# Loading K and V of a decode attention block two heads at a time, each head on half of the partitions

## Chip, core and metric

The kernel runs on one core of a Trainium2 chip. The metric is the time of one execution on the device, in microseconds (us). The core has a matrix engine (TensorE, PE in the profile, with its weight loads as PEld), a vector engine (VectorE, DVE), a scalar engine (ScalarE, ACT), GpSimd (POOL), a sync engine (SyncE, SP) that issues the DMAs here, and 16 DMA engines that carry bytes from the DRAM (HBM) to the on-chip memory of 128 partitions.

## What is computed

One token `x` (640 numbers) goes twice through an attention block A and a mixer block B, with the same weights and the same caches both times. In code cut to what matters:

```
A(x):  q = layernorm(x) @ wq                       # 32 heads of 192
       k, v = cache[head, last 4096 rows, 192]     # one K and one V head per query head
       p = softmax(q . k / sqrt(192));  o = p @ v
       return o @ wo
B(x):  x1 = x + 0 (one position: the shifted paths are zero);  return x1 + gelu(layernorm(x1) @ w3) @ w4
x = x + A(layernorm(x));  x = x + B(layernorm(x));  and both once more
```

All tensors are bf16. The last 4096 rows of one head of K, or of V, are 4096 x 192 x 2 bytes = 1,572,864 bytes (1536 KB in the profile). Nearly everything that moves is K and V: 32 heads of each, for two layers.

## The kernel before

**Loads.** On-chip memory holds 11 buffers ("cells") of 128 partitions x 12,288 bytes. One head of K or V fills one cell: `load_k` (L128 to L131) and `load_v` (L133 to L145) read it as `(p j) d -> p (j d)`, so that partition p gets 32 consecutive rows, which are 12,288 consecutive bytes in DRAM. `take` (L114) pulls the next free cell from a queue, `give` returns one. The order of all loads is written out in advance by `layer_stream` (L203): K of the next group of four heads alternates with V of the current group, and `wo`, `w3` and `w4` stand between and behind. `need` (L247) issues loads in that order. SP carries them all on one queue; each waits until the instructions that used its cell last are done. In layer 1, K of heads 0 to 6, V of heads 2 and 3 and a part of V of head 4 are not loaded again, since layer 0 keeps them on the chip.

**Scores.** Layer 0 takes its groups from head 31 downwards, layer 1 from head 0 upwards. VectorE turns each K head in four pieces in 32-bit words (`transpose_quart`, L358 to L378), PE multiplies them by the query (`scores`, L441 to L454). The query stands in `Qblk`, a block that is zero outside of the columns of one head, so the four heads of a group add into one PSUM tile (`qproj_steps`, its `block` at L430 writes the four heads with one VectorE instruction).

**Softmax.** `softmax_steps` (L471) takes maxima, exponentiates on ScalarE, turns P on VectorE (L510), swaps it into place with 16 matmuls (`swap`, L521), copies the result to `PT` on ScalarE (L524) and sums the rows (L526).

**PV.** `pv` (L558) runs 16 matmuls for each head (L567), with two columns of `PT` as weights and 384 columns of V as moving data, and then one VectorE transpose of the result (L574). `o_fold` (L576) folds four partial sums into the head's output with small matmuls and one ScalarE scaling.

**Order.** The four compute engines and SP run in the order in which the Python code records instructions (the schedule is manual); `attention` (L639 on) interleaves the next group's scores with the current group's PV. The mixer follows each layer.

The loads' source patterns, before, are one line each:

```python
t = take(("k", layer, h))
nc.sync.dma_start(t[:], A_k_cache[0, h, s0:Sk, :].rearrange("(p j) d -> p (j d)", p=P))
```

Of the kernel before, what the change touches and what calls it, by code (L numbers as in the profile page):

```python
# [17 lines left out]
P = 128  # L18
# [17 lines left out]
def kernel(  # L36
# [39 lines left out]
    NKEEP, NCELL = 7, 11  # L76
# [13 lines left out]
    cells = ctx.enter_context(tc.tile_pool(name="cells", bufs=1))  # L90
# [15 lines left out]
    kx = const.tile([P, VN], BF16, name="kx")  # L106

# [3 lines left out]
    free = deque(range(NCELL))  # L111
    cell_of = {}

    def take(key):  # L114
        i = free.popleft()
        cell_of[key] = i
        return cells.tile([P, FREE], BF16, tag=f"cell{i}", name=f"cell{i}")

    def give(key):
        free.append(cell_of.pop(key))  # L120
# [7 lines left out]
    def load_k(layer, h):  # L128
        t = take(("k", layer, h))
        nc.sync.dma_start(t[:], A_k_cache[0, h, s0:Sk, :].rearrange("(p j) d -> p (j d)", p=P))  # L130
        return t  # L131

    def load_v(layer, h):  # L133
        t = take(("v", layer, h))
        src = A_v_cache[0, h, s0:Sk, :].rearrange("(p j) d -> p (j d)", p=P)
        cut = (2 * VW,) if h == VP else (FREE - VN,) if h == VX else ()
        if layer == 1 and h in GROUPS[layer][-1][-2:]:
            cut = FREE // 2,
        i = 0
        for e in cut + (FREE,):  # L140
            kept_v = h == VP or h == VX and i > 0
            if layer == 0 or not kept_v:
                nc.sync.dma_start(v_pair(t, h, i, e - i), src[:, i:e])
            i = e
        return t  # L145
# [23 lines left out]
    def load_w3(layer):  # L169

        t = take(("w3", layer))
        src = B_w3.rearrange("(k p) f -> p k f", p=P)
        n = W3C if layer == 0 else W3C // 2
        for k in range(0, W3C, n):
            nc.sync.dma_start(t[:, k * F:(k + n) * F].rearrange("p (k f) -> p k f", f=F), src[:, k:k + n, :])
        if layer == 0:
            nc.sync.dma_start(wx_sb[:, 0:(ND - W3C) * F].rearrange("p (k f) -> p k f", f=F), src[:, W3C:, :])
        return ([t[:, k * F:(k + 1) * F] for k in range(W3C)]
                + [wx_sb[:, k * F:(k + 1) * F] for k in range(ND - W3C)])

    def load_w4(layer):

        t = take(("w4", layer))
        blocks = [t[:, k * D:(k + 1) * D] for k in range(W4C)]
        x0 = (ND - W3C) * F
        blocks += [wx_sb[:, x0 + k * D:x0 + (k + 1) * D] for k in range(NF - W4C)]
        pairs = B_w4.rearrange("(k p two) n -> p k (two n)", p=P, two=2)
        ones_ = B_w4.rearrange("(k p two) n -> p k two n", p=P, two=2)
        h = W4C // 2
        n = h if layer == 0 else h // 2  # L190
        for k in range(0, h, n):
            nc.sync.dma_start(t[:, 2 * k * D:2 * (k + n) * D].rearrange("p (k n) -> p k n", k=n), pairs[:, k:k + n, :])
        nc.sync.dma_start(blocks[2 * h], ones_[:, h, 0, :])
        if layer == 0:
            nc.sync.dma_start(blocks[2 * h + 1], ones_[:, h, 1, :])
            rest = NF // 2 - h - 1
            nc.sync.dma_start(wx_sb[:, x0 + D:x0 + D + 2 * rest * D].rearrange("p (k n) -> p k n", k=rest),
                              pairs[:, h + 1:, :])
        return blocks
# [3 lines left out]
    def layer_stream(layer):  # L203
        groups = GROUPS[layer]
        seq, later = [], []

        def k_item(hh):
            if layer == 0 or hh >= NKEEP:
                seq.append(("k", layer, hh))

        def v_item(hh):
            if (layer, hh) == (1, VC):
                return
            if (layer, hh) == (1, VP):
                later.append(("v", layer, hh))
                return
            seq.append(("v", layer, hh))

        if layer == 0:
            for hh in groups[0]:  # L220
                k_item(hh)
        for gi, cur in enumerate(groups):
            nxt = list(groups[gi + 1]) if gi + 1 < len(groups) else []
            late = gi + 2 >= len(groups)
            for i, hh in enumerate(cur):
                if nxt:
                    k_item(nxt.pop(0))
                if nxt and late and i == 2:
                    k_item(nxt.pop(0))
                v_item(hh)  # L230
                if later and seq[-1] == ("k", layer, NKEEP):
                    seq.append(later.pop())
                if layer == 0 and gi + 1 == len(groups) and i < 2:
                    seq.append(("wo", layer, groups[gi + i - 1][0] // QH))
            if gi + 2 < len(groups) and gi >= layer:
                seq.append(("wo", layer, cur[0] // QH))
        if layer == 1:
            for g in groups[-2:]:
                seq.append(("wo", layer, g[0] // QH))
        seq.append(("w3", layer))  # L240
        seq.append(("w4", layer))
        return seq
# [19 lines left out]
    ones = const.tile([P, P], F32, name="ones")  # L262
    nc.vector.memset(ones[:], 1.0)
# [16 lines left out]
    nc.vector.reduce_sum(lo[:], ident[:, 0:64], axis=AX.X)  # L280
    maskq = const.tile([P, 4], F32, name="maskq")
# [38 lines left out]
    def ln_center(x, rowsum):  # L320

        mean_ps = psm.tile([P, 1], F32, tag="psm")
        nc.tensor.matmul(mean_ps[:], lhsT=ones[:], rhs=rowsum[:, 0:1], start=True, stop=True)
# [10 lines left out]
        def total():  # L334
            var_ps = psm.tile([P, 1], F32, tag="psm")
            nc.tensor.matmul(var_ps[:], lhsT=ones[:], rhs=ssq[:, 0:1], start=True, stop=True)
# [21 lines left out]
    def transpose_quart(layer, h, q):  # L358
# [5 lines left out]
        Ku = Kn[:].bitcast(U32).rearrange("p (j y b) -> p j y b", j=NJ4, b=32)  # L364
# [4 lines left out]
        else:  # L369
            if area[0] is None:  # L370
                area[0] = take(("area", layer))
# [8 lines left out]
    def qproj_steps(c, xc, part=None, row=None):  # L380
# [6 lines left out]
        def project():  # L387
            need("wq", 0, ND - 1)
# [41 lines left out]
        def block():  # L430
            nh = n * P // Dh
            h0 = 4 * (t0 - c * QT) // NCOL
            diag = Qblk[:, c % 2].rearrange("p (h r) -> p h r", h=QH)[:, h0:h0 + nh, 0:QHEAD]
# [37 lines left out]
    def softmax_steps(n, ST_ps, sc):  # L471
# [25 lines left out]
        def spread_max():  # L497
            nb_ps = psm.tile([P, 1], F32, tag="psm")
            nc.tensor.matmul(nb_ps[:], lhsT=held["w"],  # L499
                             rhs=ones[0:1, 0:1], start=True, stop=True)  # L500
# [14 lines left out]
        def swap():  # L515
            ng = NGK // NT
            PT_ps = psm.tile([P, n, NJ4, NGK], F32, tag="psm")
            src = held["PrT"].rearrange("p (g j i) -> p i j g", g=ng, j=NJ4)
# [4 lines left out]
            PT = big.tile([P, n, NJ4 * NGK], BF16, name="PT")  # L523
            nc.scalar.copy(PT[:].rearrange("p h c -> p (h c)"), PT_ps[:].rearrange("p h j g -> p (h j g)"))  # L524
            l_ps = psm.tile([P, QH], F32, tag="psm")
            nc.tensor.matmul(l_ps[:], lhsT=ones[:], rhs=held["lh"][:], start=True, stop=True)  # L526
            held["lps"] = l_ps
            return PT
# [29 lines left out]
    def pv(layer, h, hq, PT, mid=None):  # L558
# [3 lines left out]
        NB = NJ4 * NGK // 2  # L562
        for i in range(NB):
            if mid is not None and i == NB // 2:
                mid()
            r = 32 * (i % 4)
            nc.tensor.matmul(O_ps[r:r + 2, :], lhsT=PT[:, hq, 2 * i:2 * i + 2],  # L567
                             rhs=v_pair(V, h, 2 * i * Dh, 2 * Dh), start=(i < 4), stop=(i >= NB - 4))
# [3 lines left out]
        else:  # L572
            give(("v", layer, h))
        nc.vector.transpose(o_sb[:], O_ps.rearrange("p (e a c) -> p e c a", e=2, c=NA))  # L574

    def o_fold(h, oT, rl, add=False):  # L576
        r = slice(32 * (h % QH), 32 * (h % QH) + 32)
        oT_ps = psm.tile([P, NA], F32, tag="psm")
        if not add:
            for e in range(2):  # L580
                nc.tensor.matmul(oT_ps[r, :], lhsT=Lq[:], rhs=o_sb[:, e, :, e], start=(e == 0), stop=(e == 1))  # L581
# [3 lines left out]
        nc.vector.tensor_add(o2[:], o_sb[:, 0, :, 0], o_sb[:, 1, :, 1])  # L585
# [53 lines left out]
    def attention(layer, x_cur, rs_cur, x_new, z_new, rs_new, ss_new):  # L639
# [18 lines left out]
        def S(h, half, ST_ps, hq):  # L658
# [6 lines left out]
            if half == 1 and layer == 0 and h == last_plain:  # L665
                give(("area", layer))
                area[0] = None

        def add_y(y_ps, n):
            y_new = x_new if n == 0 else sm.tile([P, ND], F32, name="y_acc")  # L670
            if n == 1:
# [5 lines left out]
                def center():  # L677
                    nm_ps = psm.tile([P, 1], F32, tag="psm")
                    nc.tensor.matmul(nm_ps[:], lhsT=ones[:], rhs=rs[:, 0:1], start=True, stop=True)
# [17 lines left out]
        qa, qb = (qproj_steps(groups[0][0] // QH, xc, part) for part in (0, 1))  # L697
# [6 lines left out]
        q1 = qproj_steps(groups[1][0] // QH, xc)  # L704
# [27 lines left out]
        for gi, cur in enumerate(groups):  # L732
            nxt = list(enumerate(groups[gi + 1])) if gi + 1 < len(groups) else []
            ST_n = None
            if nxt:
                part_max, turn_max, full_max, spread_max, turn_p, swap, recip = softmax_steps(len(cur), ST, sc)
                ST_n = next_scores()
                if layer == 1 and gi == 0:
# [3 lines left out]
                    q = qproj_steps(groups[2][0] // QH, xc)  # L742
# [17 lines left out]
                else:  # L760
# [14 lines left out]
                    if gi + 2 < len(groups):  # L775
                        q = qproj_steps(groups[gi + 2][0] // QH, xc, row=q_row if gi in rows else None)
# [33 lines left out]
            for hq, h in order:  # L810
                pv(layer, h, hq, PT, fold)
                if final:
# [5 lines left out]
                    if hq < QH - 2:  # L818
                        o_fold(h, oT, rl)
                    else:  # L820
                        def fold(h=h):
                            o_fold(h, oT, rl)
# [10 lines left out]
                elif hurry and hq == 2:  # L833
                    S(h3, 1, ST_n, q3)
                    steps = softmax_steps(len(cur), ST_n, sc)
# [7 lines left out]
                o_fold(h, oT, rl, len(groups) - 4 > gi >= 2 * layer)  # L843
# [14 lines left out]
    def mixer(layer, x_cur, z, rs_cur, ss_cur, x_new, rs_new):  # L858
# [5 lines left out]
        nc.tensor.matmul(s1_ps[:], lhsT=ones[:], rhs=rs_cur[:, 0:1], start=True, stop=True)  # L864
        s2_ps = psm.tile([P, 1], F32, tag="psm")
        nc.tensor.matmul(s2_ps[:], lhsT=ones[:], rhs=ss_cur[:, 0:1], start=True, stop=True)
# [35 lines left out]
        give(("w3", layer))  # L902
# [31 lines left out]
        give(("w4", layer))  # L934
# [51 lines left out]
```

## Time and profile before

| what | value |
|---|---|
| time, median of 3 runs (lowest, highest) | 525.11 us (524.75, 526.35) |
| span of the profiled execution | 522.9 us |
| taken as lying around the span (525.11 less 522.9) | 2.2 us |
| DMA issues, bytes read | 159, 216.47 MB |
| PE, DVE, ACT, POOL busy | 330.3, 294.6, 49.5, 4.0 us |
| one L574 transpose, one L567 matmul | 582 ns, about 510 ns |

The profiled execution's own time outside of the profiler is not given; its span is 522.9 us, and the median of the runs stands 2.2 us above it. The profile has a page with the engines' busy time, the span in 40 slices with what the DMA engines moved in each, the DMA queues, the chain of work that ended last, and groups of instructions. A list of DMA issues names each load with its size and the time from its issue to its landing. Below that list lie the records of single DMA packets, each with its size and its duration.

### The profile page before, as it was taken

Reading aid. Unit: us, or ns where it says so; the run is one execution under the profiler, and the core shown is the slowest. Engines: PE = TensorE matmul, PEld = TensorE weight load, DVE = VectorE, ACT = ScalarE, POOL = GpSimd, SP = SyncE. Lnnn points to the kernel's source line nnn. Section 1 sums busy time; section 2 is a strip of 40 time slices with the busy share of each in tenths; the row PEclk is TensorE's granted clock in tenths of the full one; section 3 lists DMA queues with packets and bytes.
Section 4 is the critical chain, followed back from the end, with each engine's and each line's share of the span. In section 5 each row is a group of like instructions: output and inputs, shape, how many; then the busy total and the mean of one; then the engine's idle time right before and its main releaser. Section 6 shows DMA issues by size and latency. Waiting matters only on the chain.

```text
span 522.9 us, 9589 instructions
## 1 busy us (share of the span) xinstructions
PE 330.3 (63%) x4146; PEld 195.5 (37%) x4146; DVE 294.6 (56%) x589; ACT 49.5 (9%) x175; POOL 4.0 (1%) x16
## 2 busy tenths in 40 slices
PE   2057668666665566767655866667675666647675
PEld 2023334333332333434333544334343333425344
DVE  2067656666574664556624264766576866654722
ACT  1000101010010100001011101001010101001011
POOL 2000000000000000000000000000000000000000
PEclk9995656567677776576555567657787865766755
DMA  8999999999999999999999999999999999999996
GB/s 345 429 424 425 423 426 427 423 424 423 427 421 428 424 422 428 423 423 423 423 399 398 388 425 427 424 424 423 426 423 424 426 423 426 421 427 425 420 410 237
DMA packets 23949, 217.08 MB, mean 415 GB/s; under 512 B 2532, under 2 KB 3044, under 8 KB 8420
## 3 DMA queue, kind: packets, MB, share of 16 engines
q1 hardware_dynamic: 23908, 216.48, 99.0%
q8 instruction: 32, 0.52, 0.4%
q14 instruction: 9, 0.07, 0.0%
HBM read 216.47 MB, written 0.00 MB: 414 GB/s over the span
## 4 chain that ended last, share of the span: by engine, by line
DMA 43%; PE 27%; DVE 25%; issue 2%; ACT 2%; SPq 1%; DVEq 0%; ACTq 0%
PE ST_ps L451 11%; DVE cell_3304 L375 9%; PE O_ps L567 8%; DVE cell_277 L375 8%; DMA cell_1925<-in_A_k_cache_dram 6%; DMA cell_4933<-in_A_k_cache_dram 5%; DMA cell_1629<-in_A_k_cache_dram 5%; DMA cell_1329<-in_A_k_cache_dram 5%; DMA cell_4637<-in_A_k_cache_dram 5%; DMA cell_5324<-in_A_v_cache_dram 5%; DMA cell_275<-in_A_k_cache_dram 4%; DVE o_sb L574 2%; DMA cell_2478<-in_A_v_cache_dram 2%; DMA cell_2690<-in_A_v_cache_dram 2%; DMA cell_5423<-in_B_w_dram 2%
## 5 line engine op out<-in xcount | busy, mean ns | idle before, releaser
L451 PEld LDWEIGHTS <-Qblk 128*16 128x16 bf16 x1536 | 86.1, 113 | 178.6 <-issue 151.1
L451 PE MATMUL ST_ps<-cell_277,Qblk 128*16 128x256 bf16 x600 | 70.1, 392 | 50.9 <-DVE cell_277 L375 34.3
L574 DVE STREAM_TRANSPOSE o_sb<-O_ps 128x384 f32<-128x384 f32 x64 | 37.2, 582 | 112.4 <-PE O_ps L567 112.3
L451 PE MATMUL ST_ps<-cell_3304,Qblk 128*16 128x256 bf16 x600 | 67.3, 382 | 43.5 <-DVE cell_3304 L375 28.3
L567 PEld LDWEIGHTS <-PT 128*2 128x2 bf16 x1024 | 47.2, 102 | 21.8 <-issue 11.3
L510 DVE STREAM_TRANSPOSE o_sb<-o_sb 128x256 bf16<-128x256 bf16 x16 | 7.1, 445 | 34.1 <-ACT o_sb L505 25.0
L582 ACT ACTIVATE oT<-oT_ps,rl 32x6 bf16<-32x6 f32 x40 | 10.3, 258 | 163.5 <-PE oT_ps L581 157.1
L581 PEld LDWEIGHTS oT_ps<-o_sb,Lq 128*32 128x32 f32 x160 | 13.2, 145 | 19.9 <-issue 16.1
L581 PE MATMUL oT_ps<-o_sb,Lq 128*32 128x6 f32 x160 | 13.9, 196 | 10.4 <-DVE o_sb L574 9.9
L587 ACT ACTIVATE oT<-oT_ps,rl 32x6 bf16<-32x6 f32 x24 | 6.2, 258 | 108.4 <-PE ST_ps L451 93.7
L405 PE MATMUL qT_ps<-xc,wq_sb 128*128 128x1 bf16 x210 | 7.2, 165 | 13.4 <-DMA wq_sb<-in_A_wq_dram 12.5
L419 DVE TENSOR_TENSOR Xq<-qT_ps,maskq 128x24 bf16<-128x24 f32 (+1 forms) x18 | 2.8, 157 | 18.3 <-PE qT_ps L405 18.3
L521 PE MATMUL PT_ps<-o_sb,Eq 128*32 128x32 bf16 x256 | 7.2, 237 | 9.2 <-DVE o_sb L510 4.0
L394 PE MATMUL qr_ps<-wq_sb,xc 128*1 128x384 bf16 x90 | 12.8, 433 | 0.0
L521 PEld LDWEIGHTS <-Eq 128*32 128x32 bf16 x256 | 5.5, 111 | 18.9 <-issue 18.8
L405 PEld LDWEIGHTS <-wq_sb 128*128 128x128 bf16 x210 | 6.8, 104 | 14.8 <-DMA wq_sb<-in_A_wq_dram 13.6
L502 ACT COPY nb_sb<-nb_ps 128x1 f32<-128x1 f32 x16 | 2.5, 159 | 97.6 <-PE nb_ps L499 97.6
L526 PE MATMUL l_ps<-lh,ones 128*128 128x4 f32 x32 | 8.5, 336 | 4.9 <-ACT PT L524 4.9
L499 PEld LDWEIGHTS nb_ps<-ones,o_sb 1*128 1x128 f32 x32 | 7.6, 292 | 7.4 <-issue 5.5
L526 PEld LDWEIGHTS l_ps<-lh,ones 128*128 128x128 f32 x32 | 7.1, 275 | 7.5 <-ACT PT L524 7.1
L499 PE MATMUL nb_ps<-ones,o_sb 1*128 1x1 f32 x32 | 8.9, 345 | 1.5 <-DVE o_sb L491 1.5
L426 PE MATMUL Qrep_ps<-Xq,Lb 128*128 128x24 bf16 (+1 forms) x18 | 3.2, 179 | 10.4 <-DVE Xq L419 10.1
(376 smaller groups left out, 533.2 us busy)
## 6 DMA issues: line engine op xcount, KB each, us to landing
wq_sb<-in_A_wq_dram SPq DMA_DIRECT2D x5, 1536.0 KB, 12.7
cell_275<-in_A_k_cache_dram SPq DMA_DIRECT2D x1, 1536.0 KB
cell_309<-in_A_k_cache_dram SPq DMA_DIRECT2D x1, 1536.0 KB, 26.4
cell_346<-in_A_k_cache_dram SPq DMA_DIRECT2D x1, 1536.0 KB, 27.1
cell_376<-in_A_k_cache_dram SPq DMA_DIRECT2D x1, 1536.0 KB
cell_444<-in_A_k_cache_dram SPq DMA_DIRECT2D x1, 1536.0 KB, 30.8
cell_503<-in_A_v_cache_dram SPq DMA_DIRECT2D x1, 1536.0 KB, 30.8
cell_505<-in_A_k_cache_dram SPq DMA_DIRECT2D x1, 1536.0 KB, 30.8
```

Of the source, the lines that this page charges most:

```text
L375: nc.vector.transpose(Tu, Ku[:, :, q * NY:(q + 1) * NY])
L394: nc.tensor.matmul(qr_ps[32 * i:32 * i + 1, :], lhsT=xc[:, kc:kc + 1], rhs=wq_sb[:, kc, t0 * P + i * N:t0 * P + (i + 1) * N], start=(kc == ...
L405: nc.tensor.matmul(qT_ps[:, tl:tl + 1], lhsT=wq_sb[:, kc, t * P:(t + 1) * P], rhs=xc[:, kc:kc + 1], start=(kc == 0), stop=(kc == ND - 1))
L451: nc.tensor.matmul(ST_ps[r:r + QW, :].rearrange("p (g i) -> p g i", g=ng), lhsT=Q[:, n, :], rhs=T4[:, :, f, :, t], start=(hq == 0 and n == ...
L499: nc.tensor.matmul(nb_ps[:], lhsT=held["w"], rhs=ones[0:1, 0:1], start=True, stop=True)
L510: nc.vector.transpose(held["PrT"], held["Pr"])
L521: nc.tensor.matmul(PT_ps[32 * m:32 * (m + 1), :, :, ng * q:ng * (q + 1)], lhsT=Eq[:, q, :], rhs=src[:, m:QW:NM], start=True, stop=True)
L526: nc.tensor.matmul(l_ps[:], lhsT=ones[:], rhs=held["lh"][:], start=True, stop=True)
L567: nc.tensor.matmul(O_ps[r:r + 2, :], lhsT=PT[:, hq, 2 * i:2 * i + 2], rhs=v_pair(V, h, 2 * i * Dh, 2 * Dh), start=(i < 4), stop=(i >= NB - 4))
L574: nc.vector.transpose(o_sb[:], O_ps.rearrange("p (e a c) -> p e c a", e=2, c=NA))
L581: nc.tensor.matmul(oT_ps[r, :], lhsT=Lq[:], rhs=o_sb[:, e, :, e], start=(e == 0), stop=(e == 1))
L582: nc.scalar.activation(oT[r, :], oT_ps[r, :], ACTF.Copy, scale=rl[r, 0:1])
```

## The change

K and V of heads 8 to 31 in layer 0, and of heads 12 to 31 in layer 1, load in pairs. One DMA brings heads h and h + 1: h to partitions 0 to 63 and h + 1 to partitions 64 to 127, 24,576 bytes on each partition, into two neighbouring cells. Those are 24 heads x 2 + 20 heads x 2 = 88 head loads, in 44 pairs. The cells become slices of one tile, `arena`, and the cell of each load comes from a list that is written out. Each of the two cells then holds one half of both heads, and what worked on a head works on such a half-half cell:

- `block` writes the query of a pair group so that one cell's scores come out for two heads, with four smaller VectorE instructions for a group instead of one. The zeros around them are at other places in pair groups, so GpSimd clears half of `Qblk` again where the kind of group changes.
- `swap_pair` takes the place of `swap`: 16 matmuls with other strides, then two ScalarE instructions that scale by 1 or 0 (`lo`, `hi`) instead of one copy, so that `PT` has twice the columns, half of them zero on each half of the partitions.
- `pv` uses four columns of `PT` as weights instead of two, adds both cells of a pair into the same PSUM rows, and transposes the result once for a pair.
- `o_fold` folds both heads of a pair behind the second.
- The last V pair of layer 1 loads in three cuts (12,288, 6,144 and 6,144 bytes of each partition); before, the last two V heads loaded in two halves each.

As built, there are 115 DMA issues instead of 159 for the same 216.47 MB. VectorE has 22 fewer of the 128x384 transposes (42 instead of 64), and of the `Qblk` writes 44 small ones and 6 of the old kind instead of 18 of the old kind, and one more of 128x1; ScalarE has 22 `PT` instructions and 5 copies instead of 16 copies; GpSimd has 4 more clears of 128x400. The numbers of matmuls and of weight loads are the same.

```diff
-    NKEEP, NCELL = 7, 11
+    NKEEP, NCELL, NSINGLE = 7, 11, (8, 12)
...
-    cells = ctx.enter_context(tc.tile_pool(name="cells", bufs=1))
+    arena = const.tile([P, NCELL * FREE], BF16, name="arena")
...
+    def is_pair(layer, h):
+        return h >= NSINGLE[layer]
+    def take(key, n=1):
+        i = plan.popleft()
+        for c in range(i, i + n):
+            free.remove(c)
+            cell_of[(*key[:-1], key[-1] + c - i)] = c
+        return arena[:, i * FREE:(i + n) * FREE]
...
     def load_k(layer, h):
+        if is_pair(layer, h):
+            return load_pair("k", A_k_cache, layer, h)
         t = take(("k", layer, h))
...
+    def load_pair(kind, cache, layer, h):
+        t = take((kind, layer, h), 2)
+        src = cache[0, h:h + 2, s0:Sk, :].rearrange("h (r j) d -> h r (j d)", r=P // 2)
+        cuts = (FREE, 3 * FREE // 2) if (kind, layer, h) == ("v", 1, H - 2) else ()
+        i = 0
+        for e in cuts + (2 * FREE,):
+            nc.sync.dma_start(t[:, i:e], src[:, :, i:e])
+            i = e
+        for e in range(2):
+            loaded[kind, layer, h + e] = t[:, e * FREE:(e + 1) * FREE]
+        return loaded[kind, layer, h]
...
+            if (layer, c) in ((0, NSINGLE[0] // QH - 1), (0, NSINGLE[0] // QH - 2),
+                              (1, NSINGLE[1] // QH), (1, NSINGLE[1] // QH + 1)) and not part:
+                nc.gpsimd.memset(Qblk[:, c % 2], 0.0)
...
+            if is_pair(layer, c * QH):
+                r = held["r"][:, :].rearrange("p (h f) -> p f h", h=nh)
+                m = blkm[:, :].rearrange("p (c g) -> p c g", c=2).unsqueeze(1).broadcast_to([P, NCOL, 2, 2])
+                for h in range(nh):
+                    v, e = h0 + h, h % 2
+                    x = QHEAD * v + 8 * (v // 2) + 2 * e
+                    rows = Qblk[:, c % 2, x:x + QHEAD].rearrange("p (f x) -> p f x", x=QW)[:, :, 0:8]
+                    nc.vector.tensor_tensor(
+                        out=rows.rearrange("p f (c g) -> p f c g", c=2)[:, :, :, 0:2],
+                        in0=r[:, :, h - e:h - e + 2].unsqueeze(3).broadcast_to([P, NCOL, 2, 2]), in1=m, op=ALU.mult)
+                return
...
+        def swap_pair():
...
+            for c, side in enumerate((lo, hi)):
+                nc.scalar.activation(PT[:, :, :, c], PT_ps[:].rearrange("p h j (g e) -> p h (j g) e", e=2),
+                                     ACTF.Copy, scale=side[:, 0:1])
...
-            nc.tensor.matmul(O_ps[r:r + 2, :], lhsT=PT[:, hq, 2 * i:2 * i + 2],
-                             rhs=v_pair(V, h, 2 * i * Dh, 2 * Dh), start=(i < 4), stop=(i >= NB - 4))
+            nc.tensor.matmul(O_ps[r:r + M, :], lhsT=PT[:, hq, i, :],
+                             rhs=v_pair(V, h, 2 * i * Dh, 2 * Dh), start=(i < 4 and not (paired and h % 2)),
+                             stop=(i >= NB - 4 and not (paired and h % 2 == 0)))
...
+        if paired and h % 2 == 0:
+            return
         nc.vector.transpose(o_sb[:], O_ps.rearrange("p (e a c) -> p e c a", e=2, c=NA))
```

## The prediction

> **What bounds the kernel now.** I read the 40 slices first, then the DMA queues, the chain that ended last, and the list of DMA issues.
>
> ```profile
> DMA  8999999999999999999999999999999999999996
> GB/s 345 429 424 425 423 426 427 423 424 423 427 421 428 424 422 428 423 423 423 423 399 398 388 425 427 424 424 423 426 423 424 426 423 426 421 427 425 420 410 237
> DMA packets 23949, 217.08 MB, mean 415 GB/s; under 512 B 2532, under 2 KB 3044, under 8 KB 8420
> ...
> q1 hardware_dynamic: 23908, 216.48, 99.0%
> ```
>
> The 16 DMA engines are busy in every slice but the first and the last, and move 423 to 428 GB/s throughout, apart from the three slices at the change of layers. So the loads bound the kernel: 424 GB/s over 16 engines is 26.5 GB/s for each engine, and one head of 1.573 MB takes 1.573 / 424 = 3.71 us. No compute engine comes near.
>
> ```profile
> PE 330.3 (63%) x4146; PEld 195.5 (37%) x4146; DVE 294.6 (56%) x589; ACT 49.5 (9%) x175; POOL 4.0 (1%) x16
> ...
> DMA 43%; PE 27%; DVE 25%; issue 2%; ACT 2%; SPq 1%; DVEq 0%; ACTq 0%
> ```
>
> The chain names PE and DVE too, but only because a load waits for the cell that they free while seven others are in flight (a load issued at 173.34 us landed 29.22 us later, eight times 3.71 us). The queue on the 16 engines never runs dry.
>
> **How many engines does a load use?** This decides the case. Each DMA engine that takes part in a load closes it with one packet of 4 bytes; the packet records hold 2,522 of these on q1. There are 159 issues. Two of them are unlike the rest:
>
> ```profile
> wx_sb<-in_A_x_dram SPq DMA_DIRECT2D x1, 1.2 KB
> out_dram<-Lb SPq DMA_DIRECT2D x1, 1.2 KB
> ```
>
> They have five rows of 256 bytes each, and all others have 128. 157 x 16 + 2 x 5 = 2,522, and with the ten rows of 256 bytes that is the 2,532 "under 512 B" of the page exactly. With 16 engines for these two it would be 2,554, with one 2,524. So the outer count of a load's access pattern sets its engines: 128 rows run on 16, five rows on five.
>
> The new load's destination still has 128 rows. Its source, `h (r j) d -> h r (j d)`, has an outer count of 2: two heads lie 6,291,456 elements apart and their 64 rows can't be joined into one step. No row of before has unlike outer counts on its two sides. The bounds are 16 engines (the destination's 128 decides) and 2 (the source's 2 decides). My reason: an engine reads and writes the same piece, so a load can hardly be cut finer than its coarser side. The nearest row, the load of `x`, is the only load with fewer than 16 source rows, and it ran on as many engines as it had rows. I take 2.
>
> [...]
>
> **The price of a pair on two engines.** One engine moves 64 rows of 24,576 bytes. The packet records have 12,288 bytes in 462 ns (median of 15,232) and 7,680 in 294 ns (1,792). Doubling gives 924 ns for 24,576 bytes, the slope between the two gives 462 + 12,288 x (168 / 4,608) = 910. I take 917: 64 x 917 = 58.7 us for a pair, where two heads took 7.42 us. Does an engine get faster when the other 14 are idle? Packets of 2,560 bytes take 106 ns with 16 or more packets in flight and 102 ns with 5 to 12, as the queue drains at the end; 1,280 bytes take 55 ns in both. So at most 4% are to be had.
>
> **The sum.** From the span I take the 88 heads at the old price and add 44 pairs at the new one. All other loads (216.47 less 138.41 MB) stay as they are, on 16 engines, and queue behind the pairs on the two busy ones as before:
> 522.9 - 88 x 3.71 + 44 x 58.7 = 522.9 - 326.5 + 2,582.8 = 2,779.2 us. With the 2.2 us by which the median of the runs exceeds the span: **2,781 us**, 5.3 times before.
>
> Does the queue stay full? A pair waits for two neighbouring cells, an added wait on SP, and behind it wait all later loads and through them everything. By the waits of the built program, at least three further loads are already in flight whenever a pair lands. One pair takes 58.7 us, in which all engines together have less than 15 us of work for two heads (PE 330.3 us for 128 head steps of K and V, 2.6 us for one; DVE 2.3). So the wait ends long before its turn, and costs nothing.
>
> **The other edits** lie under these loads. Each with its row:
> - VectorE: 22 transposes at L574 go, 22 x 582 ns = 12.8 us less. 44 small `Qblk` writes (128x24) come, between 155 ns (the 128x24 write at L419) and 247 ns (the old 128x96 one), taken at 160: 7.0 us more, while 12 old ones at 247 ns or less go, 3.0 less. Net about 9 us less of 294.6.
> - ScalarE: 22 `PT` instructions for 11 copies of 266 ns: 2.9 us more, 0.27 us on each pair group's way from P to PV.
> - GpSimd: 4 clears of 128x400, between 0.41 us (33x384, L728) and 0.77 us (128x800, L303); the `Qblk` write of that group waits for it, and scores behind that, once each.
> - PE: as many matmuls. 704 weight loads of 4 columns instead of 2: between 102 ns (2 columns) and 113 ns (16 columns), at most 7.7 us in all, beside matmuls of 510 ns. The 176 matmuls of `swap_pair` read and write with other strides: 237 ns each by the old row, at worst doubled, 42 us in all.
> - The first fold of a pair moves behind the second head: one fold of about 1 us later at the end. The tail holds 17.6 us behind the last V landing (505.28 to 522.9) and keeps them: `wo`, `w3` and `w4` still load on 16 engines behind it.
> - SP: 44 issues fewer at 0.33 to 0.49 us; it waits most of the time already.
> If the cover were gone (loads free), all these together would be some 50 us at worst; beside 58.7 us for each pair they are nothing.
>
> **Rivals.**
> 1. *All 16 engines take the pairs* (the destination's 128 decides), and the change does what it can: eight rows of 24,576 bytes on each engine, 910 to 924 ns, against sixteen of 462: 44 x 8 x 0 to 14 ns = 0 to 4.9 us less. The dip at the change of layers (three slices near 395 instead of 424) holds another 3 x 13.07 x 29 / 424 = 2.7 us that other prefetching could win. This gives 517.5 to 525, about 522 us: the other side, faster. It decides from the point where the closing packets show 16 per pair. For it: 128 partitions are written. Against: the `x` load's five.
> 2. *Sixteen engines, but the pairs stall.* A wait for two free cells lets the queue run dry. Priced at one more pair time (7.4 us) at each of the 11 pair groups: 525 + 82 = 607 us. Against: three loads in flight behind each.
> 3. *An uneven split gives 8 engines* (each head's 64 rows cut further): 16 rows each, 14.7 us for a pair: 522.9 - 326.5 + 646.8 + 2.2 = 845 us. No row shows such a cut.
>
> **How the numbers follow.** Two engines 0.87 (2,781 us); sixteen and faster or alike 0.07; sixteen with stalls 0.02; eight 0.04. For the two-engine case the low end is 4% off the pairs' 2,582.8 us (103) and 910 ns rather than 917 (20): 2,658, rounded out to 2,640. The high end takes the mean packet of 466 ns doubled, 932 ns (42 us more), and a gap of 2 us between any two pairs (88 us): 2,911, rounded to 2,920. This range holds about 0.93 of its case, 0.81 of all, so it needs no other case in it. A measurement can tell about 0.3% from no change: faster by more than that 0.05, within 0.02, slower 0.93.
>
> **What would show it.** Right: the GB/s line near 53 in the slices of pairs and 420 where single heads load, a mean DMA share near two sixteenths there; 44 pairs, or 46 issues with the last one's cuts, that close with two 4-byte packets each; rows of 24,576 bytes at 910 to 930 ns; PE, DVE and ACT with nearly the same busy time, waiting for DMAs. Wrong: slices at 420 GB/s all through (rival 1), or two-engine loads whose packets are clearly shorter than 880 ns, so that an engine alone outruns its share. A split of the 24,576-byte rows into smaller packets would move the packet count and hardly the sum.

## The result and the profile after

The changed kernel takes 2,811.34 us (median of 4 runs, 2,810.24 to 2,811.71), the kernel before 524.99 us (median of 4). The ratio is 5.3525, with a 95% interval of 5.3449 to 5.3601. 2,781 us were forecast, in a range of 2,640 to 2,920. The profiled execution has a span of 2,808.5 us. All ratios here are taken over the runs within 1.5% of their kernel's fastest.

The slices of the changed kernel, with the busy share of the DMA engines, what they moved, and the packet counts:

```profile
DMA  3111111111111111112239621111111111111113
GB/s 150 54 54 54 65 54 54 65 54 54 54 65 54 54 65 54 54 65 93 90 111 361 264 103 51 54 66 54 54 54 65 54 54 65 54 54 54 54 54 105
DMA packets 16969, 217.07 MB, mean 77 GB/s; under 512 B 1184, under 2 KB 1696, under 8 KB 6816
...
q1 hardware_dynamic: 16928, 216.47, 19.5%
```

Where pairs load, 54 GB/s move: that is two engines of about 27. Slices of 65 hold a `wo` load, which uses all sixteen by the count that follows. Only around the change of layers, where heads load singly, the rate comes back (361 GB/s in a slice). The closing packets say the same: 67 loads x 16 + 46 pair issues x 2 + 2 x 5, and ten rows of 256 bytes, make 1,184, the number "under 512 B".

Engines, as in the first part of the page, and the two longest waits for a DMA (engine and what waits, what it waits for, us in total, times, longest):

```profile
PE 325.0 (12%) x4146; PEld 187.7 (7%) x4146; DVE 285.8 (10%) x600; ACT 53.3 (2%) x186; POOL 5.7 (0%) x20
```

```profile
DVE arena L407 <- DMA arena<-in_A_k_cache_dram: 1263.9, 25, 60.4
PE O_ps L639 <- DMA arena<-in_A_v_cache_dram: 1067.4, 28, 56.2
```

The engines' work is what it was; they wait for K and V in turn, each time for up to about the time of one pair. (The chain that ended last puts 82% down to "another core or an unknown queue" here. The 40 longest of these pieces last 46 to 60 us each and stand where a pair is on its way.)

### The profile page after: what moved, and what is told of

It reads as the page before. It is cut to its first block, busy times and chain, and to the rows that moved or that the text cites. A ratio compares the mean times of both kernels' runs of the same rounds, so it can differ in the third digit from the quotient of the medians.

```text
span 2808.5 us, 9561 instructions
## 1 busy us (share of the span) xinstructions
PE 325.0 (12%) x4146; PEld 187.7 (7%) x4146; DVE 285.8 (10%) x600; ACT 53.3 (2%) x186; POOL 5.7 (0%) x20
## 2 busy tenths in 40 slices
DMA packets 16969, 217.07 MB, mean 77 GB/s; under 512 B 1184, under 2 KB 1696, under 8 KB 6816
## 3 DMA queue, kind: packets, MB, share of 16 engines
q1 hardware_dynamic: 16928, 216.47, 19.5%
HBM read 216.47 MB, written 0.00 MB: 77 GB/s over the span
## 4 chain that ended last, share of the span: by engine, by line
another core or an unknown queue 82%; PE 8%; DVE 5%; DMA 2%; issue 1%; SPq 1%; ACT 1%; DVEq 0%; ACTq 0%
DVE arena L407 4%; PE ST_ps L497 4%; PE O_ps L639 3%; DMA arena<-in_A_v_cache_dram 1%; DMA wq_sb<-in_A_wq_dram 1%; SPq L192 1%; DMA arena<-in_B_w_dram 1%; DVE o_sb L649 1%; PE l_ps L597 0%; PE nb_ps L546 0%; DVE o_sb L557 0%; ACT o_sb L552 0%; ACT PT L590 0%; DVE pm L523 0%
## 5 line engine op out<-in xcount | busy, mean ns | idle before, releaser
L407 DVE STREAM_TRANSPOSE arena<-arena 128x768 uint32<-128x768 uint32 x228 | 204.4, 946 | 1320.0 <-DMA arena<-in_A_k_cache_dram 1263.9
L497 PE MATMUL ST_ps<-arena,Qblk 128*16 128x256 bf16 x1536 | 157.8, 395 | 1277.0 <-DVE arena L407 704.5
L639 PE MATMUL O_ps<-arena,PT 128*4 128x384 bf16 (+1 forms) x1018 | 99.1, 487 | 1067.4 <-DMA arena<-in_A_v_cache_dram 1067.4
L649 DVE STREAM_TRANSPOSE o_sb<-O_ps 128x384 f32<-128x384 f32 x42 | 24.4, 581 | 1049.8 <-PE O_ps L639 1049.8
L639 PEld LDWEIGHTS <-PT 128*4 128x4 bf16 (+1 forms) x1024 | 41.5, 107 | 1092.1 <-issue 1035.8
L697 PE MATMUL yr_ps<-arena,oT 128*1 128x320 bf16 x108 | 10.8, 345 | 0.0
L597 PE MATMUL l_ps<-lh,one 128*128 128x4 f32 x32 | 8.5, 335 | 8.2 <-ACT PT L590 7.0
L552 ACT ACTIVATE o_sb<-ST_ps,nb_sb,sc 128x256 bf16<-128x256 f32 x16 | 9.0, 563 | 0.5
L546 PE MATMUL nb_ps<-one,o_sb 1*128 1x1 f32 x32 | 8.3, 325 | 1.6 <-DVE o_sb L538 1.1
L597 PEld LDWEIGHTS l_ps<-lh,one 128*128 128x128 f32 x32 | 7.1, 275 | 10.7 <-ACT PT L590 8.6
```

The costliest lines, as they stand in the source:

```text
L407: nc.vector.transpose(Tu, Ku[:, :, q * NY:(q + 1) * NY])
L497: nc.tensor.matmul(ST_ps[r:r + QW, :].rearrange("p (g i) -> p g i", g=ng), lhsT=Q[:, n, :], rhs=T4[:, :, f, :, t], start=(hq == 0 and n == ...
L552: nc.scalar.activation(out=Pr, in_=ST_ps, func=ACTF.Exp, bias=nb_sb[:, 0:1], scale=sc[:, 0:1], accum_out=lpart[:, 0:1])
L597: nc.tensor.matmul(l_ps[:], lhsT=ones, rhs=held["lh"][:], start=True, stop=True)
L639: nc.tensor.matmul(O_ps[r:r + M, :], lhsT=PT[:, hq, i, :], rhs=v_pair(V, h, 2 * i * Dh, 2 * Dh), start=(i < 4 and not (paired and h % 2)), ...
L697: nc.tensor.matmul(yr_ps[32 * i:32 * i + 1, :], lhsT=oT[:, k:k + 1], rhs=wo_t[:, k * D + i * N:k * D + (i + 1) * N], start=(k == 0), stop= ...
```

## Experiments

All eight kernels move 216.47 MB. The theory: the source's outer count of 2 confines each pair to two engines. Against it stood the pairs' cells and waits, the longer rows, the added compute, and the two distant places that one load reads.

**Sixteen engines for the pairs, other data** (`e1_outer128`).

```diff
-        src = cache[0, h:h + 2, s0:Sk, :].rearrange("h (r j) d -> h r (j d)", r=P // 2)
+        src = cache[0, h, Sk - 2 * W:Sk, :].rearrange("(r j) d -> r (j d)", r=P)
...
-            nc.sync.dma_start(t[:, i:e], src[:, :, i:e])
+            nc.sync.dma_start(t[:, i:e], src[:, i:e])
```

> The changed kernel, but each pair load reads 128 consecutive rows of 24,576 bytes of one head (its last 8192 cache rows) instead of 64 rows from each of two heads; same bytes, same cells, same waits, same compute, other data, so the output is another one. Theory A (the outer count of 2 in the source confines a pair to two engines): outer count 128, sixteen engines, eight rows of 912 ns for a pair, 7.3 us: 196.5 us of other time + 44 x 7.3 = 518 us of span, about 517 to 525 us in all; slices at 424 GB/s. Rival B (the pairs themselves cost: two free neighbouring cells to wait for, longer rows, the added compute): stays far above 525; were only the stalls of rival 2 of the prediction real, about 607 us.

Measured: 522.24 us, ratio to before 0.9954 (0.9941 to 0.9967). Its slices:

```profile
GB/s 350 437 424 438 417 438 430 428 431 417 436 426 434 421 421 430 424 423 421 424 419 381 383 427 427 425 435 421 434 428 428 429 426 428 419 440 423 427 405 203
```

The 2,289 us between this kernel and the changed one lie in the source pattern alone. Cells, waits, row length and compute of the change are all in this kernel, and cost nothing that shows.

**The same two heads, rows alternating** (`e5_alternate`).

```diff
-        src = cache[0, h:h + 2, s0:Sk, :].rearrange("h (r j) d -> h r (j d)", r=P // 2)
+        src = cache[0, h:h + 2, s0:Sk, :].rearrange("h (r j) d -> r h (j d)", r=P // 2)
```

> The changed kernel with one rearrangement of the source altered, from h r (j d) to r h (j d): the same two heads, the same bytes and the same 24,576-byte rows, but the rows of the two heads alternate on the partitions (head h on even ones, h + 1 on odd ones), which the compute behind it does not know, so the output is another one. The source's outer count is now 64 and its second count 2. Theory A: 64 and 128 both divide by 16, sixteen engines, the same 517 to 525 us as with 128 rows of one head. Rival C (it is not the order of the counts but that a load reads two distant places, or that it isn't one plain pattern): again near 2,811 us.

Measured: 522.31 us, ratio 0.9952 (0.994 to 0.9964). Its packet counts:

```profile
DMA packets 17613, 217.07 MB, mean 416 GB/s; under 512 B 1828, under 2 KB 2340, under 8 KB 7460
```

113 x 16 + 2 x 5 + 10 = 1,828: every load but the two of five rows closes on sixteen engines. Two letters changed places. The load still has two counts and still reads two places 12.6 MB apart; only the order of the counts differs (64 outside instead of 2). Rival C falls.

**The load pattern alone, in the kernel before** (`e6_before_outer2`).

```diff
+    def two_heads(cache, h):
+        b = h - h % 2
+        return cache[0, b:b + 2, Sk - W // 2:Sk, :].rearrange("h (r j) d -> h r (j d)", r=P // 2)
...
-        nc.sync.dma_start(t[:], A_k_cache[0, h, s0:Sk, :].rearrange("(p j) d -> p (j d)", p=P))
+        nc.sync.dma_start(t[:], two_heads(A_k_cache, h) if h >= (8, 12)[layer] else
+                          A_k_cache[0, h, s0:Sk, :].rearrange("(p j) d -> p (j d)", p=P))
```

(V likewise.)

> The kernel before with one part of the change alone: the loads of the same 88 heads keep their 12,288-byte rows and their cells, but each reads 64 rows from each of two heads (outer count 2 in the source; the second halves of the heads' data are not read, so the output is another one). Nothing else of the change is in it. Theory A: two engines, 64 rows of 460 ns = 29.4 us for a load, 196.5 + 88 x 29.4 = 2,787 us of span, nearly the changed kernel's. Rival B (the pairs' cells, longer rows or the compute cost the time): near 525 us.

Measured: 2,838.54 us (one run), span 2,836.8. Its packet counts:

```profile
DMA packets 22689, 217.07 MB, mean 77 GB/s; under 512 B 1272, under 2 KB 1784, under 8 KB 7160
```

69 loads remain on 128 rows or five, and 90 issues have an outer count of 2: 67 x 16 + 90 x 2 + 2 x 5 + 10 = 1,272. The pattern alone makes the slowdown; nothing else of the change is needed. The span is 50 us above the 2,787 expected; rows of 12,288 bytes took 461 ns in the median but 487 in the mean, and no run took this apart further.

**One load for each half** (`e2_two_halves`).

```diff
-            nc.sync.dma_start(t[:, i:e], src[:, :, i:e])
+            for x in range(2):
+                nc.sync.dma_start(t[64 * x:64 * (x + 1), i:e], src[x, :, i:e])
```

> The changed kernel with each pair load issued as two loads, one head each to 64 partitions, everything else alike, and the output the reference's. Outer count 64 on both sides. Theory A with engines alone: sixteen engines, four rows of 912 ns for each half, 7.3 us for a pair: 517 to 525 us. Theory A with a limit at the memory: the time also depends on which partitions the engines write at the same time, and sixteen engines on one half of the partitions get half the rate: 196.5 + 88 x 7.3 = 839 us of span, packets near 1,820 ns. [...]

Measured: 868.96, 880.43, 888.18 and 888.18 us (median of the four 884.3); ratio of the first two 1.6664 (1.6576 to 1.6751). The profile is of the first, span 867.2.

```profile
DMA  9999999999999999999999999999999999999997
GB/s 381 208 211 215 208 229 213 208 231 215 206 220 215 221 213 214 254 252 237 422 423 380 408 417 244 244 276 215 212 218 214 214 222 216 213 222 217 215 228 243
```

All engines are shown as busy from end to end, and yet they move half as much (216 GB/s between 100 and 350 us, where the run with 128 rows of one head has 427 from 30 to 255). The packet records hold 2,554 closing packets, (67 + 92) x 16 + 10, so each half runs on sixteen engines; but a row of 24,576 bytes takes 1,862 ns (median of 5,504) instead of 912. So an engine count of sixteen is not enough: these loads, which write 64 partitions each, get half the rate. The second number, 839 us of span with packets near 1,820 ns, came near (867.2 and 1,862), but the limit at the memory that it supposes was an assumption, and this run shows the halved rate without its cause.

**Four and sixteen heads in one load** (`e3_outer4`, `e4_outer16`).

```diff
+        b = min(h, H - 4)                      # 16 for e4_outer16, here and below
+        src = cache[0, b:b + 4, Sk - 2 * W // 4:Sk, :].rearrange("h (r j) d -> h r (j d)", r=P // 4)
```

> The changed kernel, but each pair load reads 32 rows of 24,576 bytes from each of four heads (outer count 4 in the source); same bytes, cells, waits and compute, other data, so the output is another one. If engines alone count: four engines, 32 rows of 912 ns = 29.2 us for a pair, 196.5 + 44 x 29.2 = 1,481 us of span. If engines that write at the same time to partitions 32 apart share one way into the memory, as the doubled packets of the two-halves run suggest (1,862 ns): the engines on partitions 0 to 31 and 32 to 63 run in step and halve each other, packets near 1,850 ns, 59 us for a pair, and the span stays near 2,800 us although twice as many engines work. [...]

Measured: 1,644.65 us (one run), span 1,642.9, between the two numbers.

```profile
GB/s 221 62 74 99 119 106 96 119 107 106 121 106 107 121 108 106 141 108 165 157 202 385 404 189 96 83 97 121 107 105 121 109 118 109 108 105 109 109 106 154
DMA packets 17061, 217.07 MB, mean 132 GB/s; under 512 B 1276, under 2 KB 1788, under 8 KB 6908
```

Four engines: 67 x 16 + 46 x 4 + 20 = 1,276. The second and third slice of 41 us move 62 and 74 GB/s, little over the 54 of two engines, and from the fourth on it is about 106, four times 26.5. In the packet records a row takes 1,892 ns (median) in the first 60 us of the span, 1,264 in the next 60, and 912 in the median after that. The first four rows start within 0.12 us of each other and the next four take 1,896 to 1,931 ns. So the start goes with the second number (packets near 1,850 ns) and the rest with the first (912). Why the rows grow shorter is not shown: the records do not name the engine of a packet, and the shared way into the memory was an assumption that no run looked at.

> As with outer count 4, but 8 rows of 24,576 bytes from each of 16 heads (outer count 16); other data, so the output is another one. Engines alone: sixteen engines, 8 rows of 912 ns, 7.3 us for a pair, about 518 us of span. With the shared way: sixteen engines each on eight consecutive partitions, those 32 partitions apart in step, packets near 1,850 ns, 14.8 us for a pair, 196.5 + 44 x 14.8 = 848 us, about as the two-halves run (867), although source and destination both divide by 16.

Measured: 876.25 us (one run), span 874.5, rows of 1,855 ns (median).

```profile
GB/s 378 210 208 212 214 223 209 207 228 214 230 213 215 225 214 212 258 265 255 422 413 395 403 371 248 220 256 224 214 218 222 217 216 218 211 216 224 221 225 186
DMA packets 17613, 217.07 MB, mean 248 GB/s; under 512 B 1828, under 2 KB 2340, under 8 KB 7460
```

113 x 16 + 20 = 1,828: every large load, the pairs too, closes on sixteen engines, as in the run with 128 rows of one head (1,828 there as well). With the same count of engines and rows of the same length that run took 522 us and this one 876. So the number of engines is not all, and here the rows do not come back to 912 ns. The loads that lost half the rate either write 64 partitions each (the halves) or read sixteen heads, 12.6 MB apart, in one load (here). Which partitions are written and which places in DRAM are read at one time the records do not show, so neither is shown to be the cause. The 848 us of span that the shared way gave came near the 874.5; that does not show the way itself.

**The change's cells and compute with short rows** (`e7_short_rows`).

```diff
+        src = [cache[0, h + x, s0:Sk, :].rearrange("(p j) d -> p (j d)", p=P) for x in range(2)]
+        cuts = (FREE, 3 * FREE // 2) if (kind, layer, h) == ("v", 1, H - 2) else (FREE,)
...
+            x = i // FREE
+            nc.sync.dma_start(t[:, i:e], src[x][:, i - x * FREE:e - x * FREE])
```

> The changed kernel with all its cells, waits and compute, but each pair load issued as two loads of 128 rows of 12,288 bytes, one for each cell, as the kernel before loads a head; the data lie otherwise than the compute expects, so the output is another one. It asks where the 0.5% came from that the change has with sixteen engines (522.2 us with 128 rows of one head). If the longer rows are it (912 ns for 24,576 bytes instead of 2 x 460): gone, within 0.3% of before, 524 to 526 us. If the fewer VectorE instructions or the cells are it: 522 us again.

Measured: 524.75 us, ratio 1.0004 (0.9995 to 1.0012). The 0.5% of the first two runs is gone, so it came from loading a pair in one load with 24,576-byte rows. Two stretches of that first run and of this one show it (the columns at the end are the granted clock, the DMA share and GB/s):

```profile
30.00:255.00 225.00, 140.55 (x1647) 81.00 (x1650) 141.51 (x258) 21.57 (x72) 0.87 (x2) 0.72 1.01 427
...
300.00:490.00 190.00, 115.57 (x1465) 66.28 (x1468) 114.02 (x219) 18.95 (x64) 1.59 (x4) 0.69 1.01 428
```

```profile
30.00:255.00 225.00, 133.73 (x1619) 75.96 (x1620) 137.32 (x253) 21.32 (x71) 0.87 (x2) 0.71 1.01 424
...
300.00:490.00 190.00, 121.27 (x1522) 68.46 (x1516) 117.36 (x224) 18.94 (x64) 1.58 (x4) 0.69 1.01 425
```

427 and 428 against 424 and 425 GB/s. In the records a long row takes 915 ns, and two short ones 2 x 463. Eight rows on each engine for 44 pairs give 44 x 8 x 11 ns = 3.9 us less, enough for the 2.5 us between the two kernels; the smaller number of loads was not tried by itself.

**The halves on two queues** (`e8_halves_two_queues`).

```diff
+            for x, q in enumerate((nc.sync, nc.gpsimd)):
+                q.dma_start(t[64 * x:64 * (x + 1), i:e], src[x, :, i:e])
```

> The two-halves kernel (one load for each head, 64 partitions each), but the second half is issued by GpSimd on its own queue, so that each DMA engine has work for both halves of the partitions at the same time; the output is the reference's. If the halves' limit is that all engines write one half of the partitions at a time, and the engines alternate between the two queues: well under the 884 us of one queue, down to 520 to 530 if they fall out of step fully. If they stay in step (all on one half, then all on the other): 850 to 890 us again, or more, as GpSimd's own work for a DMA comes on top.

Measured: 887.58 us (one run), as with one queue; rows take 1,780 ns. The hope of 520 to 530 us missed, although rows for both halves were in flight side by side. Counted in the middle of each row, with sixteen in flight: where 6 to 10 of them came from GpSimd's queue, a row took 1,666 ns (median of 1,217 rows), where none did, 1,911 (840 rows), and not one of the 5,504 rows took under 1,200. So rows for both halves in flight do not by themselves bring back the 912 ns. GpSimd's 46 issues took 510 to 521 ns each in the mean, 23.7 us in all. Which engine writes which half at one time can't be seen, as the records do not name the engines; the cause of the halved rate stays open.

A kernel with the alternating rows and a compute that knows them was not tried. By the two runs with sixteen engines and 24,576-byte rows it would win about 0.5%, an estimate.

## Why the prediction was right, step by step

- **Engines of a pair.** Two, as taken from the `x` load's five. Before the result that one load alone stood for it, and no run had unlike counts on the two sides. The closing packets of four patterns (outer counts 2, 4, 16, 64 against a destination of 128) fit without a remainder, with 2, 4, 16 and 16 engines (1,184, 1,276, 1,828 and 1,828 packets under 512 bytes). So in these four the coarser side decided. Why, no run shows: that an engine reads and writes the same piece was the author's argument, and the records show only that each row of the changed kernel's uncut pairs was one packet (5,504 of 24,576 bytes, 43 x 128).
- **Price of a pair: the one term of the sum that was off.** 58.7 us were put down, from rows of 917 ns. With half of them on each of the two engines, the rows of 24,576 bytes took 2,552.7 us, and the cuts of the last pair some 59 us more: 2,612 us, or 59.4 us for a pair, 29 us more than the 2,582.8 in all. The median row took 912 ns, but the mean 928. 273 of the 5,504 rows overlapped a packet of another load, and took 1,182 ns in the mean; the other 5,231 took 914. The sum left this out: that a pair's rows are slowed while a load on sixteen engines runs beside them. Only the upper end of the range, with rows of 932 ns, had room for it. Rows are lengthened in the runs with halves and with 4 and 16 heads too; that it is the same thing here no run shows. The slowing is mutual: rows of 7,680 bytes (13 of their 14 loads are `wo`), 298 ns in the mean before, took 426.
- **All else.** 2,808.5 less 2,612 leaves 196.5 us; 522.9 less 326.5 had given 196.4.
- **The wait for two cells.** It cost nothing, as said: in the stretches of pairs, with two rows in flight, a row starts 908 ns (median) after the last but one, and only 12 of 5,191 such steps exceed 1,200 ns. But what limited the loads in flight were the issues (the fourth pair's held SP for 57.29 us) and not the cells: when the first pair landed at about 80 us, two more were issued and the issue of a third was under way, where I had put at least three in flight (see the last section).
- **Other edits.** VectorE 285.8 us, 8.8 less (9 forecast); a small `Qblk` write 170 ns (160). ScalarE 3.8 us more (2.9): a scaled `PT` piece takes 363 ns, more than the 266 of the plain copy. A clear on GpSimd takes 435 ns, a four-column weight load 109, the strided swap matmul 235 (237 before). All of it lies under the loads, at 522 us as well as at 2,811.
- **Rival 1** was priced at 517.5 to 525 us, about 522; with sixteen engines it is 522.2. The stalls of rival 2 do not exist. Rival 3's eight engines were seen nowhere.
- From span to median it was 2.8 us, where 2.2 had been taken.
- One reading of the profile before was too narrow: its slices lie at 421 to 429 GB/s, not 423 to 428, and the last two full ones at 420 and 410. The sum goes by 424 and is not touched by it.

## What to carry to other kernels

Before a load is reshaped, look at the outer count of its access pattern on both sides. For the counts seen here (2, 4, 5, and multiples of 16) the smaller one, up to 16, was the number of DMA engines, and the packets that close each load, counted from the profile, check it. Here exchanging two dimensions in one line was worth 2,289 us, with a row order that the compute would have to be written for. After that, look at how long a row takes: sixteen engines with loads of 64 partitions (868.96 us at best, 24,576-byte rows of 1,862 ns), or with sixteen heads in one load (876.25 us, 1,855 ns), moved about 215 GB/s in the stretches of pairs, half as much as sixteen with 128 rows of one head (522.24 us, 427 GB/s) or of two heads alternating (522.31 us, 416 GB/s over the whole span), with every engine shown as busy.

## What was not expected of the hardware

**An issue can hold SP for a whole load.** SP's issues of the changed kernel (start, duration, what it loads):

```profile
3.80 73.47 SPq L154 DMA_DIRECT2D arena<-in_A_k_cache_dram  x3
77.31 57.29 SPq L154 DMA_DIRECT2D arena<-in_A_v_cache_dram  x1
134.64 57.29 SPq L154 DMA_DIRECT2D arena<-in_A_k_cache_dram  x1
192.07 57.20 SPq L154 DMA_DIRECT2D arena<-in_A_v_cache_dram  x1
249.38 57.19 SPq L192 DMA_DIRECT2D arena<-in_A_wo_dram  x1
```

With sixteen engines such an issue took 0.33 us in `e1_outer128`, 0.54 in `e4_outer16` and `e5_alternate`, and 0.47 with halves (medians); in the changed kernel SP stayed in each of the four single ones above for 57.2 to 57.3 us, about one pair's time. The third issue ends near 77 us, when about 62 of the first pair's 64 rows can be through ((77.3 - 20.9) / 0.912, as the first row starts at 20.9 us), so about two pairs, 128 rows for each of the two engines, were issued and not yet moved when SP went on: an estimate from these times. In `e6_before_outer2`, with rows half as long, the fifth issue ends at 106.0 us, when about 185 rows are through: again some 130 rows, about two loads, so in these two runs it does not go by bytes. What holds SP the traces do not show. It cost nothing here, as the two engines did not run dry in the stretches of pairs (12 of 5,191 steps from row to row exceed 1,200 ns); that a kernel that issues other work from the same engine would stand still is an inference from the 57 us, which no run tried.

**Busy is not moving.** In the sixteen-head run (876 us) and the run with halves (869 us) the DMA line shows nines at about 215 GB/s, as it does at 424 in the kernel before. The duration of one packet of a known size tells the two apart: 24,576 bytes took 1,855 and 1,862 ns there (medians), and 915 in `e1_outer128`, where 427 GB/s move.
